# Row statistics, coefficient sums and rounding copies queued at their place of the program

## The chip, the cores and the metric

The kernel runs on one core of a Trainium2 chip. The metric is the device time of one launch, in microseconds (us). Every engine of the core (PE for matmuls, DVE, ACT and POOL for vector work, SP for starting transfers) takes its instructions from a queue of its own, in order; engines meet only where one waits for a semaphore of another or of a transfer.

## The reference

The input is x of 2048 rows by 512, in float32. Four layers are added to it in turn: spectral mixing, attention with memory, and both once more.

```python
x = x + A(layernorm(x)); x = x + B(layernorm(x))
x = x + A(layernorm(x)); x = x + B(layernorm(x))

# A: real part of a two-dimensional DFT, as matmuls
a = x @ dft_hid_re.T; b = x @ dft_hid_im.T          # 512 x 512
y = dft_seq_re @ a - dft_seq_im @ b                 # 2048 x 2048

# B: 32 heads of 16, four segments of 512 rows
logits = q @ k.T * scale + mask; p = softmax(logits)
o = g * (phi(q) @ M) / (phi(q) @ z) + (1 - g) * (p @ v)
M, z = M + phi(k).T @ v, z + sum(phi(k))            # carried from segment to segment
out = concat(o) @ wo
```

The layer norm takes the mean and the variance of each row of 512; the mask is causal within a segment.

## The kernel before

**Number format.** The matmuls of full precision run as three products of rounded parts (`matmul3`, L107): a float32 operand is split into a rounded copy `hi` and a remainder `lo`, and hi·hi + hi·lo + lo·hi are summed in one PSUM bank. `split` (L95) makes the parts: the rounded copy is an ACT instruction (L99), the remainder a subtraction on DVE (L101), or on POOL where the caller asks for it. Each tensor of the trace whose name is chi, clo, xa, xb, xs, us, wdt, wq, wk, wv, wo, xT or oh is written by these lines.

**Stages.** The first spectral layer (`place_spectral` with `direct`) multiplies the normalised rows xa with blocks of the DFT matrices (`contract`, L306, tile u; four column blocks tcn of 512, eight steps k each, 48 matmuls per step). Beside it `read_pairs` (L272) loads the coefficients of step k into craw (k even) or into half of the ring sring (k odd), splits them into chi and clo, of which there are three buffers each, forms four sums of coefficient blocks (L296) in the other half of the ring, and stores them to the DRAM tensor sum; the second spectral layer reads these sums (`product`, L333, tile m), and so needs fewer products. `normalise` (L196) loads two rows of blocks, takes their statistics (`row_stats`, L133: `bn_stats` L137 and `bn_aggr` L138 on DVE, an addition L140, a power L142 on POOL), scales them (`row_scale`, L145: four small DVE steps, L147 to L150; `normal`, L157, tile xn) and splits them into xa. `split_u` (tile us) and `hidden` (tile y) finish a spectral layer with the products by wdt.

**Attention.** `prep` normalises the rows of a segment, turns them on PE (tile xnT) and splits them into xT. `proj` makes q and k in parts, `stack` and `natural_max` the row maxima of the scores: DVE reduces every score tile nat with one custom instruction (L603, tile mx), then four small steps make mparts (L619 to L626), which PE transposes (mT). `softmax_values` computes the scores again (sT), ACT forms exp (L668, L669, tile pT), POOL masks (L672), PE multiplies with the values (pv_bank). `output` (L749) scales into onat, `outproj` multiplies by wo. Each segment has eight units of ten steps.

**Order of the work.** Each of these functions is a generator whose pieces are put at numbered steps (`place`, L177). At the end all steps are run through in order (L1056 to L1059); that is the program order. For `prep` the pieces stand at t - 8 (load), t - 5 (statistics), t - 3 (scale, first xn), t and t + 2 (PE transposes). The order in which an engine gets its instructions is not the program order: a scheduler orders each engine's queue by when it expects operands to be ready, with the program order as priority and `high_priority` (L602, L618, L640) as an advance. So an instruction whose operands are ready early can stand in its queue far ahead of its place. All PE instructions are exempt: `in_order` (L83) calls `tc.keep_in_program_order` on each matmul and transpose, which ties it behind the instruction traced just before it on the same engine. This is a rule for the order of the queue and adds no wait for completion. `behind_first` (L154) does a similar thing for the first steps only: it queues an instruction behind the first row's split.

**Buffers that matter below.** chi and clo have three buffers, xt (rows, and weights before their split) four, xn two, craw two, sring one ring whose upper half all sums share.

Of the kernel before, what the change touches and what calls it, by code (L numbers as in the profile page):

```python
# [13 lines left out]
AF = mybir.ActivationFunctionType  # L14
ALU = mybir.AluOpType
# [46 lines left out]
def spectral_infini_kernel(  # L62
# [13 lines left out]
    V, A, G, T = nc.vector, nc.scalar, nc.gpsimd, nc.tensor  # L76
# [15 lines left out]
    half_neg = consts.tile([P, 2], F32, name="half_neg")  # L92
    G.memset(half_neg, -0.5)

    def split(hi, lo, src, scale=1.0, lo_engine=V, hi_engine=None):  # L95
        if hi_engine is V:
            return V.tensor_copy(hi, src), V.tensor_tensor(out=lo, in0=src, in1=hi.bitcast(F32), op=ALU.subtract)  # L97
        else:
            A.activation(hi, src, AF.Copy, scale=scale)  # L99
        if scale == 1.0:  # L100
            lo_engine.tensor_tensor(out=lo, in0=src, in1=hi.bitcast(F32), op=ALU.subtract)  # L101
        else:
            V.scalar_tensor_tensor(
                lo, src, scale, hi.bitcast(F32), op0=ALU.mult, op1=ALU.subtract
            )
# [12 lines left out]
    def pair(name, tag, bufs, dtype=F32R):  # L118
        return sb.tile([P, 2, 512], dtype, name=name, tag=tag, bufs=bufs)
# [6 lines left out]
    def load_split(dst, key, src, name, tag, bufs):  # L126
        raw = load_rows(src, "raw")
        yield
        dst[key] = w = pair(name, tag, bufs)
        split(w[:, 0], w[:, 1], raw)  # L130
        yield

    def row_stats(xts, mv):  # L133
        n = len(xts)
        for j, xt in enumerate(xts):
            st = sb.tile([P, 6], F32, name="st", bufs=2)
            V.bn_stats(st, xt)  # L137
            V.bn_aggr(mv[:, j], st)  # L138
        ve = sb.tile([P, 2], F32, name="ve", bufs=3)[:, :n]
        V.tensor_scalar_add(ve, mv[:, :, 1], EPS)  # L140
        r = sb.tile([P, 2], F32, name="r", bufs=3)[:, :n]
        G.tensor_tensor(out=r, in0=ve, in1=half_neg[:, :n], op=ALU.pow)  # L142
        return ve, r
# [10 lines left out]
    def behind_first(wanted):  # L154
        return tc.issue_after(first_row[0].ins) if wanted and len(slots_done) < 40 else nullcontext()
# [34 lines left out]
    def place_spectral(x_in, x_out, t0, end, ln_at, direct):  # L190
# [5 lines left out]
        def normalise(n):  # L196
            leads = n[0] == 0 and direct
            xt = [load_rows(x_in[i]) for i in n]
            yield
            some = slice(n[0], n[-1] + 1, max(1, n[-1] - n[0]))  # L200
            with behind_first(direct and not leads):
                ve, r = row_stats(xt, row_mv[:, some])
            yield
            row_scale(row_r[:, some], ve, r)
            for i, src in zip(n, xt):
                xn = normal(src, row_mv[:, i], row_r[:, i : i + 1])
                if not direct and i < HALF:
                    G.tensor_tensor(
                        out=xn[:, D // 2 :], in0=xn[:, : D // 2], in1=xn[:, D // 2 :], op=ALU.subtract
                    )  # L210
                xa[i] = pair("xa", "w", 16)
                engines = {"lo_engine": V, "hi_engine": V} if leads else {"lo_engine": G, "hi_engine": A}
                lo = split(xa[i][:, 0], xa[i][:, 1], xn, **engines)
                if leads:
                    first_row.append(lo[1])
            yield

        def add_rows(k):
            xt = [load_rows(x_in[i]) for i in (k, k + HALF)]
            yield  # L220
            e, o = (
                normal(xt[n], row_mv[:, i], row_r[:, i : i + 1])
                for n, i in enumerate((k, k + HALF))
            )
            a, b = slice(0, D // 2), slice(D // 2, D)
            V.tensor_tensor(out=e[:, b], in0=o[:, b], in1=e[:, b], op=ALU.subtract)
            V.tensor_tensor(out=e[:, a], in0=e[:, a], in1=e[:, b], op=ALU.add)
            V.tensor_tensor(out=o[:, a], in0=e[:, a], in1=o[:, a], op=ALU.subtract)
            xb[k] = pair("xb", "w", 16)
            split(xb[k][:, 0], xb[k][:, 1], e)  # L230
            if k % 2 == 0:
                xs[k // 2] = pair("xs", "w", 16)
            half = xs[k // 2][:, :, k % 2 * 256 : (k % 2 + 1) * 256]
            split(half[:, 0], half[:, 1], o[:, a])
            yield
# [36 lines left out]
        def read_pairs(tcn, k):  # L272
            if not ring:
                ring.append(sb.tile([P, 8, 512], F32, name="sring", tag="xT", bufs=1))
            if k % 2 == 0:
                raw = [pair("craw", "craw", 2, F32) for _ in range(2)]
            else:
                raw = [ring[0][:, 0:2], ring[0][:, 2:4]]
            halves = [slice(0, 1), slice(1, 2)] if (tcn, k) == (0, 0) else [slice(0, 2)]
            for h in halves:  # L280
                for cc in range(2):
                    nc.sync.dma_start(raw[cc][:, h], ct[cc, tcn, k, :, h])
            yield
            for cc in range(2):
                right[tcn, cc, k] = pair("chi", "chi", 3), pair("clo", "clo", 3)
            for h in halves:
                for cc in range(2):
                    hi, lo = right[tcn, cc, k]
                    with behind_first((tcn, k) == (0, 0)):
                        split(hi[:, h], lo[:, h], raw[cc][:, h])  # L290
            yield
            t = ring[0][:, 4:]
            (r0, r1), (i0, i1) = ([raw[cc][:, h] for h in range(2)] for cc in range(2))
            for j, p, q in (0, r0, i0), (1, i0, i1), (2, t[:, 0], i1), (3, t[:, 2], r1):
                with behind_first((tcn, k) == (0, 0)):
                    summed = V.tensor_tensor(out=t[:, j], in0=p, in1=q, op=ALU.add)  # L296
            if (tcn, k) == (1, 0):
                later.append(summed)
            nc.sync.dma_start(sums[tcn, k].rearrange("j p s -> p j s"), t)
            yield  # L300
# [115 lines left out]
        if direct:  # L416
            for tcn in range(TC):
                t = start + 8 * HALF * tcn
                place(2, contract(tcn), run_from(t, 4 * HALF, 2))
                for k in range(HALF):  # L420
                    place(3, read_pairs(tcn, k), [t + 8 * k - 12, t + 8 * k - 4, t + 8 * k + 3])
        else:
            t = start
            for names, tcns in PHASES:
                for tcn in tcns:
                    for n, name in enumerate(names):
                        at = run_from(t + n, HALF, len(names))
                        place(2, product(tcn, name), at)
                    for k in range(HALF):
                        for n, name in enumerate(names):  # L430
                            u = t + k * len(names) + n
                            place(3, read_block(tcn, name, k), [u - 10, u - 4])
                    t += HALF * len(names)
            u = t - 4 * 3 * HALF
            for k in range(HALF):
                place(3, add_rows(k), [u - 48 + 6 * k, u - 44 + 6 * k])
        for k in range(2 * DT):
            cc, d = k // DT, k % DT
            tag = "craw" if k < 2 else ("chi", "clo")[k % 2]
            t = end - 7 + k if k < 2 else end - 3 + (k - 2) // 2  # L440
# [13 lines left out]
    def place_attention(x_in, x_out, t0, w_at, out_at):  # L454
# [3 lines left out]
        def prep(s, n):  # L458
            xt = [load_rows(x_in[s * LT + i]) for i in n]
            yield  # L460
            mv = sb.tile([P, 2, 2], F32, name="mv", bufs=2)
            ve, r = row_stats(xt, mv)
            yield
            rr = sb.tile([P, 2], F32, name="rr", bufs=2)
            row_scale(rr, ve, r)
            for j, i in enumerate(n):
                xn = normal(xt[j], mv[:, j], rr[:, j : j + 1])
                yield
                if i == 0:
                    xT[s] = sb.tile([P, 2, DT, 512], F32R, name="xT", bufs=1)  # L470
                pt = bank("xnT", (P, DT, P))
                for d in range(DT):
                    T.transpose(pt[:, d], xn[:, d * P : (d + 1) * P], ident)
                sl = slice(i * P, (i + 1) * P)
                split(xT[s][:, 0, :, sl], xT[s][:, 1, :, sl], pt)
                if j + 1 < len(n):
                    yield
            yield
# [623 lines left out]
```

## Time and profile before

| | us |
|---|---|
| device time, median of 3 runs | 1906.43 |
| lowest and highest run | 1903.24, 1906.45 |
| the profiled execution, first to last instruction (its span) | 1911.1 |
| PE busy in it | 1809.7 |
| DVE, ACT, POOL busy in it | 1311.1, 1062.9, 512.5 |

Of the profiled execution the page gives the span alone as its time; it is 4.7 us above the median of the unprofiled runs. In the views that follow, a row of a timeline has the start (us from the span's start), the duration, the engine, the line of the code, the operation, `out<-in` by the program's tile names, shapes and a count of merged instructions; square brackets hold the idle time of the engine before it and what ended that. A row of the table by windows has the stretch, its length, the busy time of PE, PE's weight loads, DVE, ACT and POOL with their instruction counts, the granted PE clock as a share of full speed, the share of the DMA engines' time and the transfer rate. A row of the waits has who waited for whom, the total in us, how often, and the longest.

### The profile page before, as it was taken

Reading aid. Unit: us, or ns where it says so; the run is one execution under the profiler, and the core shown is the slowest. Engines: PE = TensorE matmul, PEld = TensorE weight load, DVE = VectorE, ACT = ScalarE, POOL = GpSimd, SP = SyncE. Lnnn points to the kernel's source line nnn. Section 1 sums busy time; section 2 is a strip of 40 time slices with the busy share of each in tenths; the row PEclk is TensorE's granted clock in tenths of the full one; section 3 lists DMA queues with packets and bytes.
Section 4 is the critical chain, followed back from the end, with each engine's and each line's share of the span. In section 5 each row is a group of like instructions: output and inputs, shape, how many; then the busy total and the mean of one; then the engine's idle time right before and its main releaser. Section 6 shows DMA issues by size and latency. Waiting matters only on the chain. (4 is left out here: it accounts for less than half of the span.)

```text
span 1911.1 us, 31877 instructions
## 1 busy us (share of the span) xinstructions
PE 1809.7 (95%) x10336; PEld 1301.0 (68%) x10336; DVE 1311.1 (69%) x4073; ACT 1062.9 (56%) x2292; POOL 512.5 (27%) x831
## 2 busy tenths in 40 slices
PE   7899999999899999999889999999988999999998
PEld 6678888888556656665458888787865655666654
DVE  8654545462787787777866687777558778777773
ACT  3221213331578777767664465453337877777775
POOL 4200000002345344446431000000124443434432
PEclk9999999999899999999999999999999999999998
DMA  6665555353544333434445787563444434444231
GB/s 224 233 208 199 189 191 198 115 173 121 178 125 148 118 120 115 149 119 134 134 154 181 222 251 225 164 204 127 159 150 139 144 108 134 126 133 142 91 117 45
DMA packets 165655, 296.49 MB, mean 155 GB/s; under 512 B 17776, under 2 KB 66928, under 8 KB 165488
## 3 DMA queue, kind: packets, MB, share of 16 engines
q1 hardware_dynamic: 162224, 293.68, 47.5%
q8 instruction: 81, 1.33, 0.3%
q10 hardware_dynamic: 3264, 0.79, 0.2%
q14 instruction: 86, 0.70, 0.1%
HBM read 192.95 MB, written 100.66 MB: 154 GB/s over the span
## 5 line engine op out<-in xcount | busy, mean ns | idle before, releaser
L603 DVE CUSTOM_DVE_ANT_0 junk<-nat,mask 128x512 bf16<-128x512 f32 (+3 forms) x1024 | 496.6, 485 | 203.2 <-PE nat L87 183.9
L669 ACT ACTIVATE pT<-sT 128x512 f32<-128x512 f32 x640 | 370.3, 598 | 15.0 <-ACT sT L668 2.2
L87 PE MATMUL u<-chi,xa 128*128 128x512 f32 x1024 | 321.1, 395 | 10.9 <-DVE xa L97 7.3
L672 POOL TENSOR_SCALAR_AFFINE_SELECT pT<-pT 128x256 f32<-128x256 f32 (+1 forms) x448 | 197.4, 455 | 431.5 <-ACT pT L669 366.8
L87 PE MATMUL sT<-stkq,stkk 99*128 99x256 bf16 (+3 forms) x1024 | 250.7, 307 | 17.5 <-DVE mx L603 8.8
L87 PE MATMUL nat<-stkk,stkq 96*128 96x512 bf16 (+3 forms) x1024 | 246.5, 302 | 20.8 <-DVE mx L603 12.4
L668 ACT ACTIVATE sT<-sT 128x256 f32<-128x256 f32 (+1 forms) x640 | 208.6, 334 | 63.9 <-PE sT L87 56.7
L87 PEld LDWEIGHTS u<-chi,xa 128*128 128x128 f32 x1024 | 195.4, 191 | 52.8 <-issue 7.2
L87 PE MATMUL u<-clo,xa 128*128 128x512 f32 x512 | 202.6, 396 | 9.6 <-DVE clo L101 9.6
L142 POOL TENSOR_TENSOR r<-ve,half_neg 128x2 f32<-128x2 f32 (+1 forms) x33 | 24.0, 728 | 696.5 <-DVE ve L140 692.9
L87 PE MATMUL y<-wdt,us 128*128 128x512 f32 x768 | 182.5, 391 | 1.2 <-DVE wdt L101 1.2
L87 PEld LDWEIGHTS <-stkk 99*128 99x128 bf16 x1024 | 82.6, 99 | 146.3 <-issue 127.9
L87 PEld LDWEIGHTS y<-wdt,us 128*128 128x128 f32 x768 | 143.4, 188 | 31.6 <-DVE wdt L101 2.0
L87 PE MATMUL pv_bank<-pT,vt 128*17 128x128 f32 (+3 forms) x2048 | 158.7, 440 | 1.7 <-POOL pT L672 1.6
L87 PEld LDWEIGHTS <-stkq 96*128 96x128 bf16 x1024 | 94.9, 99 | 75.9 <-issue 37.3
L87 PE MATMUL po<-wo,oh 128*128 128x512 f32 x384 | 125.7, 443 | 7.6 <-DVE oh L101 5.4
L87 PE MATMUL pvv<-wv,xT 128*128 128x512 f32 x384 | 127.0, 443 | 3.9 <-DVE mx L603 3.9
L87 PE MATMUL pqk<-xT,wq 128*128 128x512 f32 x384 | 129.9, 447 | 0.0
L87 PE MATMUL pqk<-xT,wk 128*128 128x512 f32 x384 | 127.8, 442 | 0.0
L87 PEld LDWEIGHTS u<-clo,xa 128*128 128x128 f32 x512 | 97.7, 191 | 32.5 <-DVE clo L101 12.2
L87 PEld LDWEIGHTS pv_bank<-pT,vt 128*17 128x17 f32 x2048 | 57.6, 98 | 90.7 <-issue 77.0
L99 ACT ACTIVATE clo<-cring 128x512 fp32r<-128x512 f32 x112 | 70.6, 631 | 69.1 <-DVE chi L101 37.9
(138 smaller groups left out, 3032.0 us busy)
## 6 DMA issues: line engine op xcount, KB each, us to landing
sum<-sring SPq DMA_DIRECT2D x32, 1024.0 KB
cring<-sum SPq DMA_DIRECT2D x128, 256.0 KB
stkq<-scrq SPq DMA_DIRECT2D x64, 384.0 KB
stkk<-scrk SPq DMA_DIRECT2D x64, 384.0 KB
cring<-in_ct SPq DMA_DIRECT2D x96, 256.0 KB
sring<-in_ct SPq DMA_DIRECT2D x32, 512.0 KB
xt<-mid SPq DMA_DIRECT2D x64, 256.0 KB
craw<-in_ct SPq DMA_DIRECT2D x30, 512.0 KB
```

The lines of the kernel that those rows point to most:

```text
L87: return tc.keep_in_program_order(op(*args, **kwargs))
L99: A.activation(hi, src, AF.Copy, scale=scale)
L142: G.tensor_tensor(out=r, in0=ve, in1=half_neg[:, :n], op=ALU.pow)
L603: V.tensor_tensor_reduce(junk[:, :n], src, mask[:, 512 - n :], 1.0, 3e38, ALU.add, ALU.min, dst,)
L668: A.activation(blocks, blocks, AF.Relu)
L669: A.activation(dst, ps, AF.Exp, scale=-SCALE)
L672: G.affine_select(blocks, blocks, pattern=[[0, n] for n in blocks.shape[1:-1]] + [[1, P]], compare_op=ALU.is_ge, fill=0.0, base=0, channel ...
```

## The change

Three kinds of instruction get the same tie that PE's instructions have: each is queued behind the instruction that the program traced just before it on its engine. They are the rounded copies of `split` on ACT (L99), the row statistics (L137) on DVE, and the four coefficient sums (L296) on DVE. No instruction is added, removed or altered. The remainders (L101), `bn_aggr`, the scale steps and the loads are not tied; they follow through their operands where these come from a tied instruction.

```diff
+    pin = tc.keep_in_program_order
+
     def split(hi, lo, src, scale=1.0, lo_engine=V, hi_engine=None):
         if hi_engine is V:
             return V.tensor_copy(hi, src), V.tensor_tensor(out=lo, in0=src, in1=hi.bitcast(F32), op=ALU.subtract)
         else:
-            A.activation(hi, src, AF.Copy, scale=scale)
+            pin(A.activation(hi, src, AF.Copy, scale=scale))
...
             st = sb.tile([P, 6], F32, name="st", bufs=2)
-            V.bn_stats(st, xt)
+            pin(V.bn_stats(st, xt))
             V.bn_aggr(mv[:, j], st)
...
                 with behind_first((tcn, k) == (0, 0)):
-                    summed = V.tensor_tensor(out=t[:, j], in0=p, in1=q, op=ALU.add)
+                    summed = pin(V.tensor_tensor(out=t[:, j], in0=p, in1=q, op=ALU.add))
```

## The prediction

> **What bounds the kernel now.** I read the page first, then the table by windows, then PE's own waits, then timelines at the holes that these show.
>
> ```profile
> span 1911.1 us, 31877 instructions
> PE 1809.7 (95%) x10336; PEld 1301.0 (68%) x10336; DVE 1311.1 (69%) x4073; ACT 1062.9 (56%) x2292; POOL 512.5 (27%) x831
> ```
>
> PE is busy in 95% of the span and its order is fixed, so the time is PE's work plus its holes: 1911.1 - 1809.7 = 101.4 us. A change of queue order alone can gain no more than these and what the clock loses behind them. The windows say where they are (with the longest of PE's waits behind them).
>
> ```profile
> 0.00:50.00 50.00, 39.45 (x156) 31.04 (x156) 38.93 (x90) 14.46 (x20) 23.24 (x33) 1.00 0.68 230
> 50.00:100.00 50.00, 43.24 (x176) 34.63 (x177) 34.28 (x55) 12.66 (x15) 11.82 (x8) 0.93 0.64 218
> 100.00:130.00 30.00, 26.80 (x111) 21.65 (x110) 17.68 (x27) 7.59 (x9) 0.00 (x0) 0.94 0.66 221
> 130.00:378.00 248.00, 248.00 (x1096) 205.36 (x1095) 122.25 (x160) 61.22 (x78) 0.00 (x0) 1.00 0.53 180
> 500.00:525.00 25.00, 18.90 (x112) 10.77 (x111) 20.11 (x84) 16.58 (x38) 13.00 (x20) 0.86 0.49 156
> 540.00:560.00 20.00, 17.22 (x124) 9.72 (x126) 18.97 (x71) 16.64 (x41) 8.29 (x14) 1.00 0.49 153
> 670.00:685.00 15.00, 11.12 (x51) 6.99 (x51) 12.89 (x49) 10.85 (x25) 9.82 (x15) 0.87 0.53 165
> 820.00:845.00 25.00, 22.57 (x161) 13.64 (x160) 19.79 (x80) 15.37 (x36) 14.08 (x21) 0.93 0.54 172
> 885.00:900.00 15.00, 12.66 (x85) 8.10 (x78) 11.16 (x41) 10.99 (x26) 11.76 (x17) 0.89 0.19 63
> 940.00:975.00 35.00, 27.26 (x176) 16.01 (x176) 28.30 (x110) 24.22 (x58) 17.60 (x30) 0.90 0.30 99
> 1300.00:1315.00 15.00, 13.84 (x60) 10.80 (x59) 14.49 (x29) 6.95 (x18) 0.00 (x0) 1.00 0.38 125
> 1425.00:1440.00 15.00, 11.05 (x52) 6.75 (x53) 14.49 (x56) 9.33 (x22) 6.95 (x11) 0.89 0.42 133
> 1600.00:1615.00 15.00, 11.31 (x70) 6.25 (x68) 12.22 (x38) 9.23 (x21) 8.77 (x12) 0.89 0.61 193
> ...
> PE u L87 <- DVE xa L97: 7.3, 1, 7.3
> ```
>
> Length minus the first busy time is PE's idle time, and the clock (third number from the end) has its own loss. From 130 to 378 PE never stops: nothing is to be gained in the steady first layer. The holes are at the start, where PE waits 7.3 us for the first row and then stops again, and in attention. The clock is below 1 just where PE stood: a hole is paid twice.
>
> **The change, part by part.** It adds and removes no instruction, DMA or wait; it moves an instruction in its queue if that stood ahead of the one traced before it. Where it stood behind already, nothing moves. Matching the trace's order with the code, 29 of the 64 statistics, 25 of the 128 sums and 82 of the 578 rounding copies stand ahead. Many of the copies move past a single instruction of 0.6 us, for which I take nothing: PE has no wait there.
>
> *Start, 0 to 130.* After the first matmul PE idles 10.55 - 7.3 = 3.3, then 6.8 and 3.2, and the clock loses 0.07 x 50 + 0.06 x 30 = 5.3: 18.6 us in all. Two timelines show its making.
>
> ```profile
> 51.12 0.63 ACT L99 ACTIVATE xa<-xn 128x512 fp32r<-128x512 f32 x1 [4.24 <-DVE xn L159]
> 51.66 1.04 ACT L99 ACTIVATE chi<-sring 128x1024 fp32r<-128x1024 f32 x1
> ...
> 52.75 0.57 PE L87 MATMUL u<-chi,xa 128*128 128x512 f32 x1 [3.25 <-ACT chi L99]
> ...
> 104.16 1.29 DVE L296 TENSOR_TENSOR sring<-craw 128x512 f32<-128x512 f32 x2 [6.04 <-DMA sum<-sring]
> 105.98 1.22 DVE L101 TENSOR_TENSOR clo<-sring,chi 128x1024 fp32r<-128x1024 f32 x1
> ...
> 107.25 0.50 PE L87 MATMUL u<-clo,xa 128*128 128x512 f32 x1 [3.21 <-DVE clo L101]
> ```
>
> At 51 ACT stands 4.24 us before a copy of rows for a later step, and the chi that PE needs now is behind it. At 104 DVE stands 6.04 us because a sum wants the ring that the last store still reads; the clo that PE needs is behind the sum. Tied, the xa goes behind this chi, and the sums behind the low parts of their own step. Both holes (6.5 us, and the half clock that follows) should go. What is late next: the sums of step k now wait for xn of the rows of k + 1, and stand ahead of clo of k + 1. DVE's work per step is some 9 us (four sums 2.6, two clo 2.45, statistics, scale and xn of two rows about 3.8, by the rows here and below), against 48 matmuls in 10.9 us (1096 in 248 us). So the start stays tight on DVE, and the second step, whose chi now follows the copies of two rows, may start some 1.3 us later (two copies of 0.63). Of 18.6 I take **8 back**, with bounds 0 (DVE sets the same pace) and 15.
>
> *Steady first layer.* The sums come later by some 16 us, and with them the release of the raw blocks:
>
> ```profile
> 131.60 2.62 DVE L296 TENSOR_TENSOR sring<-sring 128x512 f32<-128x512 f32 x4 [1.26 <-DMA sring<-in_ct]
> 148.15 1.23 DVE L101 TENSOR_TENSOR clo<-sring,chi 128x1024 fp32r<-128x1024 f32 x1 [3.47 <-ACT chi L99]
> ```
>
> The block used at 148 had landed by 131.6. Behind the change its sums end near 152.0, not 134.2, and SP issues the store of the sums and then the next load into this half, instead of the load right after 149.4. This half is used every second step, each 10.9 us (48 of the window's 1096 matmuls in 248 us): the next load landed near 131.6 + 21.7 = 153.3 so far. Behind 2.6 us of sums and a store that two of these loads make up in size I put it at 161, and it is needed at 148.15 + 21.7 = 169.9. Cover: 8 us. Cost **0**; if the cover were gone, each of 24 steps would wait.
>
> *Attention's start.* Statistics of segments whose place is far behind stand between the reductions:
>
> ```profile
> 501.26 0.69 DVE L137 BATCH_NORM_STATS2 st<-xt 128x6 f32<-128x512 f32 x1
> ...
> 505.44 0.68 DVE L137 BATCH_NORM_STATS2 st<-xt 128x6 f32<-128x512 f32 x1
> 506.05 0.41 DVE L619 SCALAR_TENSOR_TENSOR mparts<-mx 128x16 bf16<-128x16 f32 x1
> 509.82 0.55 DVE L159 TENSOR_SCALAR xn<-xt,mv,rr 128x512 f32<-128x512 f32 x1
> ...
> 508.13 0.33 PE L87 MATMUL mT<-ident_b,mparts 128*80 128x128 bf16 x1 [2.93 <-DVE mparts L626]
> ```
>
> Four statistics (first and last shown), 4 x 0.68 = 2.7 us, go ahead of the mparts for which PE stands 2.93 us, and the clock of 500 to 525 is 0.86 (3.5 us lost). All four move behind 539. The same picture stands at 1425 to 1440 (idle 3.95, clock 1.65). I take **8 back** for both, between 3 (the hole only shrinks) and 13.
>
> *Rows scaled early.* At 674 to 679 scale steps and both xn of a segment whose transposes come much later run amid the reductions; tied statistics take them along:
>
> ```profile
> 674.69 0.93 DVE L147 TENSOR_TENSOR rt<-r 128x2 f32<-128x2 f32 x1
> 676.54 1.03 DVE L150 TENSOR_TENSOR rr<-r,rt 128x2 f32<-128x2 f32 x1
> 678.11 1.28 DVE L159 TENSOR_SCALAR xn<-xt,mv,rr 128x512 f32<-128x512 f32 x2
> ```
>
> That is 3.2 us of DVE in the window 670 to 685, which loses 3.9 idle and 2.0 by the clock; 820 to 845 and 1600 to 1615 are of the same kind (2.4 + 1.8, 3.7 + 1.7). Of 15.5 in all I take **6 back** (bounds 0 and 12), since the reductions themselves remain.
>
> *Copies of the second spectral layer.*
>
> ```profile
> 887.81 0.63 ACT L99 ACTIVATE xa<-xn 128x512 fp32r<-128x512 f32 x1 [2.23 <-POOL xn L208]
> ...
> 891.16 0.38 PE L87 MATMUL nat<-stkk,stkq 96*128 96x128 bf16 x2 [2.25 <-ACT pT L669]
> ```
>
> ACT stands 2.23 us before a copy that is not due, and PE 2.25 us for the exp behind it. The copies move 30 us back. 885 to 900 loses 2.3 + 1.7, 940 to 975 7.7 + 3.5. I take **4 back** (0 to 10).
>
> *What the tie costs in attention.* The statistics now run at their place, and the chain behind them is short of time: statistics, power on POOL, four scale steps, xn, then PE's transposes. For the second segment:
>
> ```profile
> 539.45 0.28 DVE L778 TENSOR_TENSOR onat<-on,rec 128x128 f32<-128x128 f32 x1
> ...
> 542.33 0.60 PE L87 MATMUL xnT<-ident,xn 128*128 128x128 f32 x4
> ...
> 3.48 0.69 DVE L137 BATCH_NORM_STATS2 st<-xt 128x6 f32<-128x512 f32 x1 [3.48 <-DMA xt<-in_x]
> 6.10 0.55 DVE L159 TENSOR_SCALAR xn<-xt,row_mv,row_r 128x512 f32<-128x512 f32 x1
> ```
>
> The tied statistics start behind 539.7; PE wants xn at 542.3, 2.6 us later. The chain takes 3.2 us on a free DVE for one row (3.48 to 6.65) and 9.1 in the busy one (501.26 to 510.37). So PE, tied to its order, stands there 1 to 6.5 us. DVE is 95% busy in 540 to 560, but the standing PE also frees it: I take 4.2, and 1.8 for the clock as in the holes above. Twice (both attentions) **12 lost**, bounds 2 and 20. For the third segment the tie is a reduction at 637.2 and the transposes stand at 646.2:
>
> ```profile
> 637.21 0.69 DVE L603 CUSTOM_DVE_ANT_0 junk<-nat,mask 128x512 bf16<-128x512 f32 x1
> ...
> 646.18 0.60 PE L87 MATMUL xnT<-ident,xn 128*128 128x128 f32 x4
> ```
>
> Nine us is about what the chain takes in the busy DVE, so the later segments lose little: I take 3 for them, bounds 0 and 8.
>
> *End of the second spectral layer.* Two wdt copies and eight us copies come back to 1293 to 1305, where DVE is busy 14.49 of 15 and PE idles 1.2: **1.5 lost**.
>
> Sum: 8 + 8 + 6 + 4 - 12 - 3 - 1.5 = 9.5 us gained, on the profile's 1911.1. The median of the runs is 4.7 lower; I take the same 9.5 from it: 1906.4 - 9.5 = 1896.9, say **1897**.
>
> [...]
>
> **Rivals.** (a) *The chain is on time:* the scale steps slip between the reductions and the 12 are not lost: 1885, to 1880 with a better start. For it: DVE has short holes at 540 to 543. (b) *Nothing:* the untied neighbours close up in the same pattern and gains and losses cancel: 1906. (c) *Slower: the chain is late at each place.* With 9.1 us of chain the second segment's first pair costs 6.5 + 2; its second pair, tied behind the first pair's second xn, I estimate at 4 + 2 from the same chain: some 14 per attention, 28 in all, and the start returns 2 instead of 8. Then 2 + 8 + 6 + 4 - 28 - 3 - 1.5 = -12.5: 1919. [...] (d) *Loads late:* the cover of 8 us at 161 is not there and 24 steps lose 1 us each: 1921 to 1930. Against it: PE never stands in 130 to 378 and the DMA engines are busy 0.53.
>
> **How the numbers follow.** Forecast (1888 to 1902) 0.50, (a) 0.16, (b) 0.11, (c) 0.20, (d) 0.03. A measurement here tells about 0.2% (3.8 us) from no change. Faster: 0.66; same: 0.11; slower: 0.23. The range leaves out the far half of (c), (d) and the best of (a): 1880 to 1916.
>
> **What would show it.** Right: no idle of PE above 2 us at 49 and 104 and a clock near 1 from 50 to 130; no statistics before 530 in attention; mT at 508 without its 2.93. The cost shows as a new wait of xnT for xn near 540 and 1465. Wrong if PE shows holes in 130 to 378, if the first 130 us take as long as before, or if xnT's waits sum to over 25 us.

## The result, and the profile after

Five runs of the changed kernel gave 1899.65 us (1895.19 to 1900.75), five of the kernel before 1906.45 (1903.24 to 1909.97): a ratio of **0.9953, 95% interval 0.9935 to 0.9971**, or some 9 us less. The profiled execution took 1895.19 us with a span of 1893.5. Single executions stray: the profile of before is 17.6 us longer than that of after, twice what the runs differ by. A run's time is 1.7 us more than its span (1895.19 against 1893.5), so the profile of before stands some 6.4 us above the median of its runs, and that of after is the shortest of its five. Sizes below that come from two profiles are those of these two executions, and good to some microseconds for the kernels.

The head of the page for the kernel after:

```profile
span 1893.5 us, 31918 instructions
PE 1802.0 (95%) x10336; PEld 1296.0 (68%) x10336; DVE 1305.9 (69%) x4073; ACT 1056.0 (56%) x2292; POOL 521.2 (28%) x831
```

PE's holes are 1893.5 - 1802.0 = 91.5 us, 9.9 less than the 101.4 of before, and PE's own busy time is 7.7 less. The windows of after, in the columns of the prediction's table, at the same places of the program (13 to 26 us earlier behind the first hundred):

```profile
0.00:50.00 50.00, 40.66 (x166) 32.81 (x167) 40.70 (x78) 14.05 (x19) 21.74 (x30) 1.00 0.66 216
50.00:100.00 50.00, 49.73 (x214) 39.21 (x213) 41.24 (x67) 16.38 (x22) 22.15 (x12) 1.00 0.69 226
100.00:130.00 30.00, 30.00 (x134) 24.84 (x133) 19.25 (x29) 5.77 (x6) 0.00 (x0) 1.00 0.70 226
130.00:366.00 236.00, 236.00 (x1043) 195.42 (x1042) 113.45 (x151) 58.17 (x73) 0.00 (x0) 1.00 0.59 191
485.00:503.00 18.00, 17.25 (x114) 10.59 (x114) 14.29 (x60) 15.49 (x38) 10.65 (x16) 0.97 0.60 176
518.00:540.00 22.00, 15.22 (x97) 8.99 (x96) 18.96 (x71) 12.96 (x31) 7.32 (x12) 0.78 0.41 121
625.00:640.00 15.00, 12.61 (x97) 8.26 (x96) 13.98 (x51) 11.41 (x27) 8.35 (x12) 1.00 0.60 194
655.00:670.00 15.00, 14.11 (x105) 9.00 (x101) 11.22 (x47) 13.60 (x32) 8.74 (x14) 1.00 0.35 104
750.00:765.00 15.00, 12.61 (x86) 8.31 (x85) 13.02 (x43) 9.84 (x23) 8.47 (x12) 0.89 0.60 189
807.00:832.00 25.00, 25.00 (x188) 15.68 (x187) 18.36 (x84) 19.54 (x46) 12.69 (x23) 1.00 0.48 149
918.00:953.00 35.00, 26.39 (x171) 14.66 (x171) 28.22 (x104) 24.80 (x59) 18.05 (x31) 0.86 0.31 100
1441.00:1461.00 20.00, 13.21 (x90) 8.18 (x89) 17.52 (x66) 11.72 (x28) 6.85 (x11) 0.77 0.42 133
1550.00:1565.00 15.00, 12.61 (x87) 8.51 (x86) 12.64 (x44) 9.87 (x23) 7.36 (x11) 0.89 0.58 183
```

In the first 130 us PE stops for the first row (7.3 us) and for the first low part (2.0 us), as in the kernel before, and then hardly at all, at a clock of 1.00. The steady layer is untouched. The early half of attention's start (485 to 503) and the places of the rows scaled early (655, 807) are nearly full. In exchange there are stretches that were better before: 518 to 540 and 1441 to 1461 at a clock of 0.78 and 0.77, and three times 12.61 busy of 15. PE's own waits name them (in total, times, longest):

```profile
PE xnT L87 <- DVE xn L161: 12.7, 9, 3.5
PE pM L87 <- DVE oh L103: 9.0, 4, 2.2
...
PE u L87 <- DVE xa L99: 7.3, 1, 7.3
PE mT L87 <- DVE mparts L628: 6.4, 3, 3.4
PE xnT L87 <- DVE rec L761: 5.1, 2, 2.5
```

The transposes of attention's rows (xnT) and a matmul pM that wants the remainder oh have no such rows among the waits of before; together they now wait 26.8 us. The wait put down to rec is one for the rows too: the xn before it ends at 535.90, rec at 535.99, and PE starts at 536.05. (The lines of after are two higher than those of before from L94 on.)

The two traces have the same instructions, so I took the end of the same instruction in both and its difference: the shift. This table holds it for each kernel against the profile of before (us; the columns are times in before; negative is earlier).

| kernel | 130 | 203 | 525 | 553 | 673 | 710 | 800 | 954 | 1420 | 1452 | 1507 | 1600 | 1865 |
|---|---|---|---|---|---|---|---|---|---|---|---|---|---|
| after | -15.6 | -15.6 | -21.7 | -15.3 | -11.9 | -17.9 | -13.3 | -22.9 | -20.0 | -25.5 | -17.0 | -13.4 | -13.3 |
| sums alone | -3.4 | -3.4 | -4.4 | -4.4 | -3.0 | -4.0 | -4.1 | -6.7 | -6.4 | -5.5 | -5.4 | -6.0 | -5.3 |
| copies alone | -4.9 | -4.9 | -5.1 | -4.7 | -4.8 | -6.3 | -6.3 | -11.8 | -8.5 | -8.2 | -6.1 | -6.6 | -7.1 |
| statistics alone | -16.2 | -13.4 | -20.1 | -12.7 | -5.5 | -11.9 | -5.4 | -13.0 | -9.0 | -14.8 | -5.0 | -0.8 | -0.7 |
| statistics, first spectral layer | -15.4 | -10.3 | -9.5 | -10.3 | -9.9 | -11.1 | -11.1 | -15.3 | -15.0 | -13.9 | -13.9 | -14.2 | -12.8 |
| statistics, both spectral layers | -15.8 | -12.8 | -13.7 | -13.7 | -12.9 | -13.3 | -13.3 | -21.2 | -19.0 | -21.2 | -21.0 | -21.0 | -20.4 |
| change, attention's free | -15.7 | -15.7 | -15.5 | -15.7 | -15.0 | -15.2 | -15.2 | -25.0 | -21.1 | -19.9 | -18.1 | -18.7 | -18.6 |
| after, second profile | -15.5 | -15.5 | -21.6 | -15.5 | -9.4 | -15.3 | -10.6 | -19.9 | -16.6 | -22.3 | -14.2 | -10.5 | -10.3 |
| before, second profile | 0.0 | 0.0 | 0.5 | 0.5 | 0.5 | 0.8 | 0.8 | 0.2 | 0.8 | 0.6 | 0.6 | 0.2 | 1.0 |

The two profiles of the change part by up to 3 us behind 553, so a difference of that size between two rows says little by itself, unless a hole is shown for it.

### The profile page after: what moved, and what is told of

The parts are those of the page before. It is cut to its first block, busy times and chain, and to the rows that moved or that the text cites. A ratio compares the mean times of both kernels' runs of the same rounds, so it can differ in the third digit from the quotient of the medians.

```text
span 1893.5 us, 31918 instructions
## 1 busy us (share of the span) xinstructions
PE 1802.0 (95%) x10336; PEld 1296.0 (68%) x10336; DVE 1305.9 (69%) x4073; ACT 1056.0 (56%) x2292; POOL 521.2 (28%) x831
## 4 chain that ended last, share of the span: by engine, by line
PE 71%; DVE 15%; issue 5%; ACT 5%; DMA 2%; POOL 1%; SPq 0%; DVEq 0%; ACTq 0%; POOLq 0%
PE u L87 14%; PE m L87 9%; PE y L87 9%; PE pqk L87 8%; PE pv_bank L87 7%; PE sT L87 6%; PE nat L87 6%; DVE junk L605 5%; PE pvv L87 4%; PE po L87 3%; DVE clo L103 2%; PE pM L87 1%; DVE chi L103 1%; ACT pT L671 1%; PE pm L87 1%
## 5 line engine op out<-in xcount | busy, mean ns | idle before, releaser
L87 PE MATMUL sT<-stkq,stkk 99*128 99x256 bf16 (+3 forms) x1024 | 252.8, 309 | 12.2 <-DMA stkq<-mt 5.0
L87 PE MATMUL nat<-stkk,stkq 96*128 96x512 bf16 (+3 forms) x1024 | 248.7, 304 | 11.9 <-DVE mx L605 8.9
L87 PE MATMUL pv_bank<-pT,vt 128*17 128x512 f32 (+3 forms) x2048 | 152.7, 437 | 0.0
L103 DVE TENSOR_TENSOR chi<-cring,chi 128x512 fp32r<-128x512 f32 x112 | 78.7, 703 | 42.1 <-ACT chi L101 40.2
```

Source lines behind the costliest of these rows:

```text
L87: return tc.keep_in_program_order(op(*args, **kwargs))
```

## The experiments

**Two theories.** The prediction's: three separate gains, each with its own instruction. The sums' tie frees the low parts at 104, the copies' tie the rounded copy at 51 and those of the second spectral layer, and the statistics' tie gains and loses in attention. The rival: one kind sets the order, and the others follow it. A statistic that runs ahead makes its row ready, then the row's scale, its xn and its copy xa run ahead too, and all of these stand in front of due work.

**One kind tied at a time.**

```diff
 sums alone: only the four sums keep pin(...); copies and statistics as before
 copies alone: only the activation in split keeps it
 statistics alone: only bn_stats keeps it
```

> Only the four coefficient sums (L296) are tied to their place. My theory, that the three ties act at different holes: the stop of DVE before the sum at 104 (6.04 us) and PE's hole of 3.21 us with its half clock go, and the holes at 49, 53, 68 and 81 stay: PE is 4 to 6 us ahead of before at 130, nothing changes in attention, 4 to 6 us faster in all. Rival, that the start is set by the sums alone: PE is about 15 us ahead at 130, as with all three ties (15.6 us in the profile of the change), and the run is faster than the change, since it has none of the waits of xnT.

> Only the rounding copies on ACT (L99) are tied. My theory: PE's hole of 3.25 us at 49 with its half clock goes, that at 104 stays; PE is 5 to 7 us ahead at 130; near 889 the hole of 2.25 us goes, with its clock 4 us more; 8 to 11 us faster in all. Rival (sums alone set the start): nothing ahead at 130, 4 us faster in all at most.

> Only the row statistics (L137) are tied. My theory: the start is within 3 us of before. In attention the stages give what the profile of the change shows against before: 6.6 + 3.9 us gained at the two starts, 6.3 + 4.5 + 5.5 gained where rows were scaled early, 7.7 + 6.8 lost at the second segments and 3.1 + 4.6 + 4.4 + 4.7 lost at the later ones: 27 gained, 31 lost, 0 to 6 us slower in all. Rival, that the statistics' tie is itself worth its place: 5 us faster or more.

The kernel before ran beside them once more, as if it were a changed one:

> The kernel before, unchanged, for a second profile of it. Time within 0.2% of before. The span of its profile tells how far one profiled execution strays: the first one, 1911.1 us, is 4.7 above the median of the runs, and the difference of the two profiles shown so far (17.6 us) is twice that of the runs. If the second span is near 1904, the excess of the first is chance of that execution, and the place where the two drift apart says which stage strays.

Measured against the runs of before on the same chip: sums alone 0.9994 (0.9982 to 1.0007), copies alone 1.0002 (0.9991 to 1.0013), statistics alone 0.9990 (0.9973 to 1.0006), before again 0.9986 (0.9974 to 0.9999). The last of these is the same kernel, so 0.1% is what this measurement gets wrong by itself; none of the three ties alone is told from no change, and the 4 to 6 and 8 to 11 us expected of the sums and the copies did not come. (The profile of copies alone is the shortest of its 11 runs, and its shift of -7.1 at 1865 is not borne out by them; that of statistics alone is the second longest of its 12.) The stages say more. Sums alone still stops PE for both parts, at 37 to 41 and again at 67 to 70:

```profile
67.08 0.49 PE L87 MATMUL u<-chi,xa 128*128 128x512 f32 x1 [2.99 <-ACT chi L101]
70.42 0.80 PE L87 MATMUL u<-clo,xa 128*128 128x512 f32 x1 [2.84 <-DVE clo L103]
```

Copies alone still stops it for the low part:

```profile
26.96 0.50 PE L87 MATMUL u<-clo,xa 128*128 128x512 f32 x1 [3.05 <-DVE clo L103]
...
55.94 0.50 PE L87 MATMUL u<-clo,xa 128*128 128x512 f32 x1 [3.93 <-DVE clo L103]
```

With the statistics alone, the second 50 us have no hole at all:

```profile
0.00:50.00 50.00, 40.03 (x167) 32.36 (x168) 37.06 (x82) 15.23 (x20) 16.45 (x29) 1.00 0.69 232
50.00:100.00 50.00, 50.00 (x222) 41.25 (x221) 35.19 (x65) 15.89 (x21) 16.32 (x12) 1.00 0.75 246
```

At 130 statistics alone is 16.2 us ahead, as much as the change, without a tied sum or copy. There the prediction's theory of the holes at 49 and 104 falls. But the order that it saw in the sums exists: behind 130 statistics alone loses 2.8 us again, most of it where a sum that waits for the ring stands in front of a due low part:

```profile
158.02 1.29 DVE L298 TENSOR_TENSOR sring<-craw 128x512 f32<-128x512 f32 x2 [5.18 <-DMA sum<-sring]
159.23 1.22 DVE L103 TENSOR_TENSOR clo<-sring,chi 128x1024 fp32r<-128x1024 f32 x1
...
160.50 0.50 PE L87 MATMUL u<-clo,xa 128*128 128x512 f32 x1 [1.55 <-DVE clo L103]
```

In the kernel after, ACT's copies and chi follow one another without a stop between them, while DVE still stands before a sum that wants the ring:

```profile
51.90 1.15 ACT L101 ACTIVATE xa<-xn 128x512 fp32r<-128x512 f32 x2 [8.17 <-DVE xn L161]
52.96 1.99 ACT L101 ACTIVATE chi<-craw 128x1024 fp32r<-128x1024 f32 x2
...
97.59 1.89 DVE L298 TENSOR_TENSOR sring<-sring 128x512 f32<-128x512 f32 x3 [4.33 <-DMA sum<-sring]
```

The stop for the ring, which I took for the cause of the hole at 104, is still 4.33 us long and costs PE nothing, since 50 to 130 is all but full (79.73 of 80) at the clock 1.00: what counts is what stands behind the stop.

**Where the statistics' tie pays.** Statistics alone still had 13.4 us at 203, and 0.7 at 1865. So two kernels tie them in parts: in the first spectral layer only, with nothing else tied; and the whole change with attention's statistics free. A third gives the tied rows more time: their statistics three places of the program earlier. The changed kernel ran again with them.

```diff
+    def row_stats(xts, mv, tie=pin):
-            pin(V.bn_stats(st, xt))
+            tie(V.bn_stats(st, xt))
 first spectral layer alone (copies and sums as before; untied by default, so attention's free):
-            ve, r = row_stats(xt, row_mv[:, some])
+            ve, r = row_stats(xt, row_mv[:, some], tie=pin if direct else (lambda i: i))
 attention's free, in prep:
-            ve, r = row_stats(xt, mv)
+            ve, r = row_stats(xt, mv, tie=lambda i: i)
 three places earlier, for s > 0:
-[t - 8, t - 5, t - 3, t, t, t + 2]
+[t - 11, t - 9, t - 6, t, t, t + 2]
```

> Only the row statistics of the first spectral layer are tied. The theory formed from the three single ties: the statistics alone set the pace of the start (13.4 us ahead at 203 with their tie alone, 3.4 with the sums' and 4.9 with the copies'), and their tie in attention gives the gain back. So PE is 13 us ahead at 203 and stays so to the end: 10 to 14 us faster, more than the change. Rival: what is gained at the start is chance of the one profiled execution and not in the runs; then within 4 us of before.

> The change with the statistics of attention's rows (prep) left untied; those of both spectral layers, the copies and the sums stay tied. Theory: 15.6 us ahead at 130 as in the change; no wait of xnT for xn in attention (the change has 12.7 us of it), and the hoisted statistics' holes at 505 and 1432 and the early rows' at 678 and 1605 are back. By the stages of the change, attention's ties gain 10 + 12 and lose 31, so 5 to 9 us faster than the change. Rival, that the two sides of attention are equal: as fast as the change within 2 us.

> The change with all its ties, and for segments 1 to 3 the load, the statistics and the first scaling of prep placed 11, 9 and 6 steps ahead of the transposes instead of 8, 5 and 3. Theory: the loss in attention is lack of time between the tied statistics and the transposes; with twice the steps the waits of xnT go from 12.7 + 5.1 us to under 5 and the waits of the following matmuls (pM, 9.0 us) shrink; 10 to 20 us faster than the change. Rival, that DVE's load itself costs PE wherever the statistics stand: the holes move some us earlier and the time is that of the change within 4 us.

> The change, unchanged, on the same chip as the other three and with more runs than so far: 6 to 11 us faster than before, and a second profile whose stages show which of the first one's differences hold. Were the first interval chance, the single ties' result (none of them differs from before) would be the measure, and this run within 4 us of before.

First spectral layer only: 0.9945 (0.9926 to 0.9964), as much as the whole change, which gave 0.9951 (0.9934 to 0.9967) on this chip. Attention's free: **0.9903 (0.9887 to 0.9920)**, 1889.65 us; it beats both kernels, and its interval and the change's do not touch. In attention the tied statistics lose some 9 us net (0.0048 of 1909.6, the median of before on this chip).

Three places earlier: 0.9941 (0.9924 to 0.9959), not told from the change, so a lack of places is not shown as the cause, and the 10 to 20 us expected of it did not come. Its trace says why it didn't help at the second segments. Rows of DVE and PE:

```profile
513.57 0.54 DVE L161 TENSOR_SCALAR xn<-xt,mv,rr 128x512 f32<-128x512 f32 x1
...
518.27 0.69 DVE L139 BATCH_NORM_STATS2 st<-xt 128x6 f32<-128x512 f32 x1
...
521.37 0.60 PE L87 MATMUL xnT<-ident,xn 128*128 128x128 f32 x4
...
523.17 0.88 DVE L150 TENSOR_TENSOR rt<-rt,ve 128x2 f32<-128x2 f32 x1
...
524.49 0.55 DVE L161 TENSOR_SCALAR xn<-xt,mv,rr 128x512 f32<-128x512 f32 x1
...
526.73 0.54 DVE L161 TENSOR_SCALAR xn<-xt,mv,rr 128x512 f32<-128x512 f32 x1
...
527.41 0.87 PE L87 MATMUL xnT<-ident,xn 128*128 128x128 f32 x3 [3.73 <-DVE xn L161]
```

The first row is in time now (xn at 513.57, transposed at 521.37 without a wait). But the next pair's statistics and scale steps moved ahead as well, to 518 to 524, in front of two xn in DVE's queue, and PE stands 3.73 us for the second of these. The wait moved by one row. In the later segments the earlier places did help: this kernel has no wait of pM for oh, though xnT waits there 1.9 us instead of 1.2, and by the shifts these segments lose 12.2 us against 15.5 in the change. Three microseconds are less than the runs can tell.

**Which segments, and what the other ties add.** Four more kernels: the change with attention's statistics tied only in its first two segments, or only in its last two; the statistics of both spectral layers alone; and attention's free without the copies' tie.

```diff
 first two / last two segments tied, in prep:
+            ve, r = row_stats(xt, mv, tie=pin if s < 2 else (lambda i: i))
+            ve, r = row_stats(xt, mv, tie=pin if s > 1 else (lambda i: i))
 both spectral layers' statistics alone: attention's free, and pin(...) taken off the copies and the sums
 no copies: attention's free, and pin(...) taken off the activation in split
```

> The change with the attention statistics tied only in the first two segments of each layer (s of 0 and 1), free in the later two. Theory: the later segments' tied statistics alone cost the 15 to 17 us read from the stage shifts, the first two gain 11.7 and lose 15. Then this kernel is near the one with all attention statistics free, less the first two's net loss of 3 us: shift at 1865 of about -15 us, ratio to the kernel before about 0.992; the shifts at 525 and 553 should be -22 and -15 as in the change, and nothing be lost from 553 to 900. Rival: the loss of a segment is caused by what is moved in the segments before it, and frees only move it: then holes of 2 us for xnT or pM come back in the later segments and the ratio is that of the change, 0.995.

> The change with the attention statistics tied only in the last two segments of each layer (s of 2 and 3). Theory: it keeps the start's 15.6 us, has neither the early rows' gain of 6 at 525 nor the loss of 7 behind it, and loses the 15 to 17 us of the later segments: holes of 2.24 us for oh near 628 and 753, shift near -3 at 1865, ratio about 0.998. Rival: tied statistics cost only where the segment before was tied too; then the ratio is that of the kernel with all attention statistics free, 0.990.

> Only the statistics tied, and only in the two spectral layers: no copy and no sum. Theory: the statistics set the order of the start and the copies that of the second spectral layer: shift -10 at 203 to 553 as with the first layer's statistics alone, about -15 at 954 as there, ratio about 0.994. Rival: the second layer's statistics bring the 9 us that the kernel with all attention statistics free gains from 553 to 954: shift -19 or more at 954, ratio 0.991 to 0.992.

> The change with the copies and the attention statistics free: sums and the spectral layers' statistics tied. Theory: the copies are worth about 5 us at the start of the second spectral layer and 2 us or less at that of the first: shift -13 to -15 at 203 to 553, about -20 at 954, ratio 0.9925. Rival: with the statistics tied the copies' place follows from theirs, so their own tie adds nothing: ratio 0.990, shift -25 at 954.

| kernel | median us | ratio to before | 95% |
|---|---|---|---|
| first two segments tied | 1896.41 | 0.9929 | 0.9914 to 0.9944 |
| last two segments tied | 1897.37 | 0.9930 | 0.9916 to 0.9945 |
| statistics of both spectral layers alone | 1892.58 | 0.9906 | 0.9892 to 0.9921 |
| attention's free, no copies | 1890.31 | 0.9898 | 0.9881 to 0.9914 |

Compared by their ratios, since the medians of before differ (1908.72 here, 1909.56 beside attention's free), each half of attention's ties costs about 0.0026 over attention's free (0.9903), and the two halves together the 0.005 that the change loses: they add up. My figure for the last two segments (0.998) was wrong in its sum, for I had charged them the later segments' 15 us and had left out that the same ties give some back (673 to 710 in the table). PE's waits place the two costs apart. First two segments tied:

```profile
PE xnT L87 <- DVE xn L161: 13.0, 4, 3.5
```

Last two tied:

```profile
PE pM L87 <- DVE oh L103: 9.0, 4, 2.2
...
PE xnT L87 <- DVE xn L161: 5.3, 5, 1.2
```

The copies' and the sums' ties add nothing to the statistics of the spectral layers that the runs can show (0.9906, 0.9898 and 0.9903, each inside the others' intervals). The traces show one thing more for the sums: without their tie PE stops behind 130 for a low part (1.69 us with both layers' statistics, 1.97 with the first's), and the shift shrinks by 203 to 12.8 and 10.3; with the sums tied and the copies free it stays at 15.8. The gain at the second spectral layer, which I had given to the copies, also comes with the statistics: with the first layer's alone, ACT and PE still stand there as before, ACT for a row's xn and PE for the exp queued behind that row's copy:

```profile
875.26 0.63 ACT L101 ACTIVATE xa<-xn 128x512 fp32r<-128x512 f32 x1 [2.23 <-POOL xn L210]
...
878.62 0.38 PE L87 MATMUL nat<-stkk,stkq 96*128 96x128 bf16 x2 [2.26 <-ACT pT L671]
```

With both layers' statistics tied that hole is gone, and from 800 to 954 the shift grows by 7.9 us against 4.2. The copies alone close it as well (-6.3 at 800, -11.8 at 954): either tie holds the same queue.

## Why the prediction came out right

The time forecast was 1897, the runs give 1899.65; in the ratio it is 9 us gained against 9.5. The gains came 21.7 us larger than forecast (47.7 against 26) and the losses 17.7 us larger (34.2 against 16.5). That these two errors nearly cancel is luck. Each term from the shifts of after:

- **Start:** forecast 8, bounds 0 to 15; measured 15.6. The holes at 49 and 104 went, as did the half clock (0.50 in 54 to 58 and in 109 to 111 of before, 1.00 in 50 to 130 of after). DVE did not set the same pace, and the second step was not late. The 2.0 us for the first low part, which the prediction counted among what might go, stayed. The failed step is the cause: "Tied, the xa goes behind this chi, and the sums behind the low parts of their own step" describes the order rightly, but the ties that I named for it gave only 4.9 and 3.4 alone, and the statistics alone 16.2 by 130. The sums' tie then keeps some 3 of these behind 130.
- **Steady first layer:** forecast 0; the shift stays at -15.6 from 203 to 384. The loads were in time and rival (d) is out.
- **Attention's starts:** forecast 8; measured 6.2 and 5.5 (492 to 525, 1420 to 1452). The statistics now stand at 517.93, which is 539.7 less the shift, as forecast.
- **Rows scaled early:** forecast 6, bounds 0 to 12; measured 6.0 (673 to 710), 4.8 (1600 to 1635) and 4.4 (831 to 864): 15.2. The last of them belongs to the second spectral layer's rows, since the kernel with attention's free has it too. I took the reductions to be the limit; without the scale steps among them, 807 to 832 is full.
- **Copies of the second spectral layer:** forecast 4; measured 5.2 (864 to 954), but by the statistics or the copies, not by the copies only.
- **Second segments:** forecast 12 lost; measured 7.2 (525 to 581) and 8.6 (1452 to 1507): 15.8. The new wait of xnT for xn is where the prediction put it. The rows below show the chain that I had reckoned with, 517.93 to 524.15, or 6.2 us to the first xn, inside the 3.2 to 9.1 that I gave; PE stands for 3.55 of it.
- **Later segments:** forecast 3, bounds 0 to 8; measured 2.6, 4.6, 3.6 and 4.7 (638 to 673, 766 to 800, 1536 to 1600, 1692 to 1726): 15.5. **This term was mis-sized most.** The step that failed is "Nine us is about what the chain takes in the busy DVE, so the later segments lose little": xnT indeed waits only 1.2 us, but I followed only those who wait for the chain, and not what is queued behind it. Behind the scale steps stands the remainder oh, for which PE's pM waits 2.24 us, four times (9.0 in all).
- **End of the second spectral layer:** forecast 1.5 lost; measured 2.9 (954 to 1420), and at another place: a hole of 1.47 us for a chi at 1031.

The sum of these, 15.6 + 11.7 + 15.2 + 5.2 - 15.8 - 15.5 - 2.9 = 13.5, is the shift at 1865 to 0.2. The second profile of the change gives 15.5, 12.0, 14.9, 4.8, -16.5, -16.9 and -3.3 for the same terms, so their sizes hold to 1.5 us. The 4.3 us that the after profile gains behind 1865 need not be the change's: the kernel before, profiled again, gained 3.3 there, from 1.0 late to 2.3 early.

The rows of after behind the two costs, DVE, POOL and PE of one stretch each:

```profile
517.93 0.69 DVE L139 BATCH_NORM_STATS2 st<-xt 128x6 f32<-128x512 f32 x1
...
522.83 0.88 DVE L150 TENSOR_TENSOR rt<-rt,ve 128x2 f32<-128x2 f32 x1
...
524.15 1.85 DVE L161 TENSOR_SCALAR xn<-xt,mv,rr 128x512 f32<-128x512 f32 x2
...
524.75 1.11 PE L87 MATMUL xnT<-ident,xn 128*128 128x128 f32 x4 [3.55 <-DVE xn L161]
...
627.59 1.16 POOL L545 TENSOR_TENSOR parts<-rem,parts 128x512 bf16<-128x512 f32 x1
627.65 1.11 DVE L149 TENSOR_TENSOR rt<-r 128x2 f32<-128x2 f32 x1
...
628.79 0.33 DVE L150 TENSOR_TENSOR rt<-rt,ve 128x2 f32<-128x2 f32 x1
629.15 0.17 DVE L151 TENSOR_SCALAR rt<-rt 128x2 f32<-128x2 f32 x1
...
629.44 0.69 DVE L103 TENSOR_TENSOR oh<-oT,oh 128x512 fp32r<-128x512 f32 x1
630.27 0.93 PE L87 MATMUL pM<-vt,pkn 128*128 128x136 f32 x6 [2.24 <-DVE oh L103]
```

The first four: the chain at its tied place, too late for the transposes. The others: oh starts as soon as three scale steps let it, and the first two of these took 1.44 us between them, where 0.16 us each is the median of the 33 of their line.

Of the rivals, (a) is out: the chain is late, with 17.8 us of xnT's waits. (b) is out, since the interval ends at 0.9971. That a hole is paid twice held for seven of the eight holes of 2.24 us in the two profiles of the change, which took clock with them (last section). In (c) the price of attention came true, 31.3 us measured against 28 + 3, though half of it lies in the later segments and waits for oh; what (c) had wrong is what comes back, 2 at the start against 15.6 and 6 for the rows against 15.2. By xnT's waits alone it stayed under the 25 us that I had named as the sign. Attention's free shows what the change gives without that price, 1889.65.

**Open:** statistics alone (0.9990) is worth 16 us less than the statistics of the spectral layers alone (0.9906), but the change only 9 us less than the change with attention's free. So the ties of sums or copies save some 7 us once attention's statistics are tied, though without these the runs show nothing for them. The first layer explains 2 to 3 us of lead at 203 in both cases (13.4 against 15.6, 12.8 against 15.7), so not the difference between them. Set against the second profile of the change, statistics alone falls behind little by little through attention (2.1 us less ahead at 203, 5.2 at 800, 9.6 at 1865), and no run tells which of the two kinds of tie holds it there. The 2.5 us by which the first layer's statistics alone fall short of both layers' at 203 are no loss of the start: both are ahead alike at 130 (15.4 and 15.8), and the difference is nearly all clock, 0.91 against 1.00 in 150 to 170, behind the stop for the low part.

## What to carry to other kernels

Find the instruction at the head of a chain that runs ahead, and tie that one: here the row statistics drew scale steps, rows and copies on two engines after them, the tie of the copies added nothing to theirs, and that of the sums closed a hole of 1.6 to 2.0 us that the runs are too coarse to show. Measure such a tie stage by stage: the same one gave 18 us in the two spectral layers and took back 9 in attention, where DVE is nearly full (18.97 of 20 us in 540 to 560 of before) and PE wants the row a few microseconds later (2.6 at the second segment), and three places more did not cure that. When pricing a tie, list what is queued behind the moved instructions as well as what waits for their results: the largest error here was an instruction that had nothing to do with the chain but stood behind it.

## What was not expected of the hardware

**Short DVE steps that last until a POOL instruction ends.** Of the 99 two-input scale steps (rt, rr and row_r, one or two columns wide) in the trace of after, 15 took over 0.25 us, up to 1.11, and each of the 15 began while a POOL instruction was under way and ended within 0.02 us of its end; so did all 18 such steps of before, the longest of 1.30 us. None of the 84 short ones lies inside a POOL instruction. The row pair at 627 shows one: POOL to 628.75, DVE to 628.76. Of the 33 scale steps with one input two took 0.38 us in after, and they too ended within 0.03 us of a POOL instruction's end. All these steps had begun and yet ended with POOL's, so DVE and POOL meet here without a wait for a semaphore, unlike what the first section says of the engines; why they do is not shown. It decided in the later segments: the two steps of 1.11 and 0.33 us at 627 stand ahead of the oh for which pM waits 2.24 us, and the 3 us forecast for these segments had no such wait in it.

**The same hole with and without a loss of clock.** Single holes of 2.24 us stand in 625 to 640, 750 to 765, 1550 to 1565 and 1676 to 1691 of the first profile; the clock of the first window is 1.00, that of the others 0.89. In the second profile of the change the first of them costs too:

```profile
625.00:640.00 15.00, 12.59 (x82) 8.41 (x85) 13.27 (x44) 10.07 (x24) 8.78 (x13) 0.89 0.54 168
```

Where the clock is lost, it drops to half behind the hole: in the first profile it is 0.50 from 756 to 758 and 1.00 again from 760 to 765, while behind the hole at 628 to 630 it is 1.00 throughout, from 629 to 640. What sets the drop off is not shown. The same hole cost clock in one execution and not in the other, and 2.24 us was enough in seven of eight cases. A hole's price in clock is therefore in part a chance, as far as these two profiles go, and 4.8 us in 518 to 540 (0.22 of 22) was nearly three times the 1.8 that I had put there.
